# Fourier mixing and a SoLU block on one core: edge columns to GpSimd and ScalarE, and an earlier start for the products of w_in

## The chip, the cores and the metric

The kernel runs on one core of a Trainium2 chip, as one launch. A core has a matrix engine (TensorE, PE in the profile), a vector engine (VectorE, DVE), a scalar engine (ScalarE, ACT), a general engine (GpSimd, POOL) and a fifth (SyncE, SP) that here only issues transfers. They run side by side, each through its own queue, and wait for each other through semaphores. Sixteen DMA engines move data between DRAM and the on-chip memory; transfers issued by SyncE are the queue q1 of the profile, the gathers issued by GpSimd are q0. The metric is the device time of the launch in microseconds (us); lower is better.

## The reference

A real array x of 8 sequences, 3136 positions and 256 features goes through two Fourier transforms, of which the real part is kept. The result, 25088 rows of 256, goes through a SoLU block with a layer norm:

```python
X = np.fft.fft(np.fft.fft(x, axis=1), axis=2).real.astype(np.float32)
h = X.reshape(25088, 256) @ w_in                    # 256 x 1024
e = np.exp(h - np.max(h, axis=-1, keepdims=True))
sm = e / (np.sum(e, axis=-1, keepdims=True) + 1e-09)
solu = h * sm
mu = np.mean(solu, axis=-1, keepdims=True)
var = np.mean((solu - mu) ** 2, axis=-1, keepdims=True)
ln = (solu - mu) / np.sqrt(var + 1e-06) * g_ln
out = (ln @ w_out).astype(np.float32)               # 1024 x 256
```

x and g_ln are float32. w_in and w_out arrive as float64, so the kernel has to turn them into float32 itself.

## The kernel before

**Tiling.** The eight sequences are handled as four pairs (class Pair). The 3136 positions are split into 49 x 64, and the transform along them is done in two steps. `transform1` multiplies by the table F (49 points), `transform2` by the table T (64 points). The symmetry of a real transform is used: x is added to its mirror image along the sequence (`add_mirror`, from a copy xb that GpSimd gathers in reversed order), and then features d and 256-d are added and subtracted into a tile y (`fold_features`). The transform along the features is not done on the data: its table Q is multiplied into w_in beforehand. So the first product of the SoLU block uses Wi = Q x w_in, and w_mid holds one more row for the middle feature.

**Chunks.** A pair is processed in NC = 8 chunks c of CH = 4 positions each. For the first pair (`first`), a chunk is loaded (`load`: xa by SyncE, xb by GpSimd), mirrored and folded whole. The edge columns have no partner in the fold: column 0 gets only the mirror add (L147) and is then copied to y together with column 128 (L165). Chunk 7 also has y0, from position 0. For later pairs the work is spread over the main loop in halves (`fold_part`). The tiles y have two buffers, so the fold of chunk c can start when `transform1` of chunk c-2 has read its y. `transform1` runs twice per chunk: two matmuls (columns 0 to 128, and 129 to 255) into a PSUM bank, then a ScalarE copy (L220) to a tile z. After each chunk, rows of z go to DRAM (zd, by `keep`). When all eight chunks are there, `turn` reads them back as g in another layout, and `transform2` can start. A float32 matmul shows as two records in the profile.

**Weights.** w_in comes in four pieces of 512 KB (`piece_in`): pieces 0 and 1 are its first 128 rows (w_in[0]), 2 and 3 its other 128 rows (w_in[1]). Each is turned from float64 to float32 by integer steps: `exponent_in` takes the exponent on VectorE (L586) and clamps it with three ScalarE activations (`confine`, L610, L612, L614); `narrow_in` builds the float on VectorE (L586, L627, L630, L636). w_out goes the same way later (`exponent_out`, `narrow_out`). `product_in(h, parts)` computes a half h of Wi: parts 0 and 2 are the contributions of w_in[0] to the two column halves, 1 and 3 those of w_in[1]. `keep_in` (L694) copies the finished product out of PSUM on ScalarE. `product_in(KD)` is the product for w_mid, from a table that `mid` prepares. `scale_out` transposes the gain g_ln through PSUM bank 2, and ScalarE copies it out (L711). `mean_out(0)` and `mean_out(1)` sum w_out over its rows on TensorE (L737), for the mean of the layer norm.

**Order.** `tc.manual_schedule()` is in force: every engine executes its instructions in the order in which the program writes them. The start of the program is a hand-written sequence: loads, then the loop over the eight chunks of the first pair, in which the narrowing of the weights is interleaved, then the products that are left, then the second transform of units 0 and 1. A unit is one k1 of one pair. After that the main loop goes over 4 x 25 units: `up` (L281, h), `even` and `join`, `expo`, `product`, `square`, the transposition, and the second product (`down`, or `Down` with seven block products in place of eight). The transfers of the start are issued by SyncE in this order: idx, pieces 0 and 1, xa of chunk 0, F, the gain, piece 2, xa of chunks 1 and 2, piece 3, xa of chunks 3 to 5, Q; then, as buffers come free, xa of chunks 6 and 7, w_out, T and the keeps. The six first gathers of xb are issued by GpSimd meanwhile, before it clears T.

**PSUM.** `result(i)` gives bank i % 4 of four banks. `transform1` of the first pair uses them in turn, two per chunk.

Of the kernel before, what the change touches and what calls it, by code (L numbers as in the profile page):

```python
# [9 lines left out]
FP32 = mybir.dt.float32  # L10
I32 = mybir.dt.int32
U32 = mybir.dt.uint32
ALU = mybir.AluOpType
# [10 lines left out]
PR = 2 * N1  # L24
ZR = 4 * NK
CH = 4
NC = NH // CH
# [17 lines left out]
def kernel(  # L45
# [19 lines left out]
    nc = tc.nc  # L65
    B, S, D = x.shape
    FF = moe_w_in.shape[1]
    KF = FF // P
    KD = D // P
# [8 lines left out]
    xpool = ctx.enter_context(tc.tile_pool(name="xpool", bufs=2))  # L78
# [17 lines left out]
    ident = const.tile([P, P], FP32, name="ident")  # L96
# [9 lines left out]
    def result(i):  # L106

        return banks[i % 4]
# [9 lines left out]
    def load(pr, c, room=None):  # L118

        r = slice(pr.p * PR, (pr.p + 1) * PR)  # L120
        rows = PR if pr.p else P
        if room is None:
            xa = xpool.tile([P, CH, D], FP32, tag="xa", name="xa")
            xb = xpool.tile([P, CH, D], FP32, tag="xb", name="xb")
        else:
            xa, xb = (t.rearrange("p (l d) -> p l d", d=D) for t in room)
        nc.sync.dma_start(out=xa[0:rows], in_=x_pn[r.start : r.start + rows, c * CH + 1 : (c + 1) * CH + 1, :])
        i = pr.p * NC + c
        nc.gpsimd.indirect_dma_start(
            out=xb[0:rows].rearrange("p l d -> p (l d)"), out_offset=None, in_=x_g,  # L130
            in_offset=bass.IndirectOffsetOnAxis(ap=idx[0:rows, i : i + 1], axis=0))
        xa, xb = xa[0:PR], xb[0:PR]
        x0 = None
        if c == NC - 1:
            x0 = xpool.tile([PR, 1, D], FP32, tag="x0", name="x0", bufs=1)
            nc.sync.dma_start(out=x0, in_=x_pn[r, 0:1, :])
        pr.raw[c] = (xa, xb, x0)

    def add_mirror(pr, c, engine, part=None):

        xa, xb, _ = pr.raw[c]
        rows = (0, CH) if part is None else (part * CH // 2, (part + 1) * CH // 2)
        r = slice(rows[0], min(rows[1], CH - 1 if c == NC - 1 else CH))
        a, rb = xa[:, r, :], xb[:, ::-1, :][:, r, :]
        i = engine.tensor_tensor(out=a[:, :, 1:D], in0=a[:, :, 1:D], in1=rb[:, :, D - 1 : 0 : -1], op=ALU.add)  # L145
        if part is None:
            engine.tensor_tensor(out=a[:, :, 0:1], in0=a[:, :, 0:1], in1=rb[:, :, 0:1], op=ALU.add)  # L147
        return i

    def fold_features(o, i):  # L150
        up, down = i[:, :, 1:128], i[:, :, 255:128:-1]
        nc.vector.tensor_tensor(out=o[:, :, 1:128], in0=up, in1=down, op=ALU.add)
        nc.vector.tensor_tensor(out=o[:, :, 129:256], in0=up, in1=down, op=ALU.subtract)

    def fold(pr, c):

        xa, _, x0 = pr.raw.pop(c)
        pr.y[c] = xpool.tile([PR, CH, D], FP32, tag="y", name="y")
        sides = [(pr.y[c], xa)]
        if c == NC - 1:  # L160
            pr.y0 = xpool.tile([PR, 1, D], FP32, tag="y0", name="y0", bufs=1)
            sides.append((pr.y0, x0))
        for o, i in sides:
            fold_features(o, i)
            nc.vector.tensor_copy(out=o[:, :, 0:129:128], in_=i[:, :, 0:129:128])  # L165

    def fold_part(pr, c, part):

# [66 lines left out]
    def transform2(pr, k1, bank=0):  # L235

        i, k = divmod(k1, KG)
        g = pr.g[i]  # L240
        table = T[0][:, :, k, :] if i == 0 else T[1][:, :, k1 - KG, :]
        ps = result(bank)[:, 0 : KD * P]
        for h in range(KD):
            o = ps[:, h * P : (h + 1) * P].rearrange("p (b k) -> p b k", b=2)
            nc.tensor.matmul(o, g[:, k, h * P : (h + 1) * P], table,  # L245
                             start=(h == 0), stop=True, skip_group_check=True)
        return ps
# [324 lines left out]
    NW = 512  # L572
# [25 lines left out]
    def confine(unit, here=False, parts=(0, 1, 2)):  # L598

        if unit is None:  # L600
            return
        if here:
            bits(unit, unit, -896.0, ALU.add, 0.0, ALU.max)
            bits(unit, unit, 255.0, ALU.min, 2.0 ** 23, ALU.mult)
            return

        u = unit.bitcast(FP32)
        for i in parts:
            if i == 0:
                nc.scalar.activation(out=u, in_=unit, func=ACT.Relu, bias=limits[:, 0:1])  # L610
            elif i == 1:
                nc.scalar.activation(out=u, in_=u, func=ACT.Relu, bias=limits[:, 1:2], scale=-1.0)  # L612
            else:
                nc.scalar.activation(out=unit, in_=u, func=ACT.Identity, bias=limits[:, 2:3], scale=-(2.0 ** 23))  # L614
# [24 lines left out]
    class Weights:  # L639
# [43 lines left out]
        def product_in(self, h, parts=range(4), ps=None):  # L683
# [6 lines left out]
                nc.tensor.matmul(ps[:, fs], lhsT, self.w_in[c][:, fs], start=(c == 0), stop=(c == KD - 1))  # L690
            return ps

        def keep_in(self, h, ps):
            nc.scalar.copy(w_mid if h == KD else Wi[:, h, :], ps)  # L694

# [61 lines left out]
    def ahead(pr, i, work, after=None):  # L757

        for c in range(NC):
            a = i - SUMS[pr.p][c]  # L760
            if work == "load" and (i == (pr.p - 1) * NK and c < 2 and (c or pr.p == 1) or a == 2 and c + 2 < NC):
                load(pr, c if a != 2 else c + 2)
            if work == "mirror" and a in (0, 1):
                behind(add_mirror(pr, c, nc.gpsimd, a), after or units[i - 1])
            if work == "fold" and a in (1, 2):
                fold_part(pr, c, a - 1)
# [24 lines left out]
    with tc.manual_schedule():  # L791
        pairs = [Pair(p) for p in range(NP)]
        first, weights = pairs[0], Weights()
# [10 lines left out]
        weights.piece_in(1)  # L804
        load(first, 0)
        nc.sync.dma_start(out=F, in_=f_tab)
        weights.load_gain()
        weights.piece_in(2)
        for c in range(1, 6):
            load(first, c, rooms.get(c))  # L810
            if c == 2:
                weights.piece_in(3)
        weights.load_tables()
        nc.vector.memset(ones, 1.0)
        nc.vector.memset(neg_half, -0.5)
        bits(top_bit, neg_half[:, 0:1].bitcast(I32), 31, ALU.logical_shift_right, 31, ALU.logical_shift_left)
# [6 lines left out]
        for c in range(NC):  # L823

            if c == 0:
                weights.narrow_in(0)
                weights.narrow_in(1)
            elif c == 1:
                weights.narrow_in(2)
            add_mirror(first, c, nc.vector)  # L830
            if c == 0:
                weights.exponent_in(2)
            fold(first, c)
            if c == 1:
                weights.exponent_in(3)
            elif c == 2:
                weights.narrow_in(3)
            if c == NC - 1:
                for i in range(2):
                    weights.exponent_out(i)  # L840
                confine(weights.units[0], True)
                weights.narrow_out(0)
            if c + 6 < NC:
                load(first, c + 6)
            if c == 3:
                weights.place_out()
                for i in range(2):
                    weights.load_out(i)
                weights.load_table(0)
                weights.scale_out()  # L850
            for s in range(CH // 2):
                if c == NC - 1:
                    confine(weights.units[0], parts=(s,))
                transform1(first, c * CH // 2 + s)
            if c == 3:
                weights.mid()
            elif c == 5:
                weights.keep_in(0, weights.product_in(0))
            elif c == 6:
                odd = weights.product_in(1, (0, 1))  # L860

        turn(first, 0, nc.sync, 0, 2)
        turn(first, 0, nc.gpsimd, 2, KG)

        weights.product_in(1, (2, 3), odd)
        middle = weights.product_in(KD)
        confine(weights.units[0], parts=(2,))
        for i in range(2, 4):
            weights.exponent_out(i)
        weights.keep_in(1, odd)  # L870
        confine(weights.units[1])
        weights.keep_in(KD, middle)

        units = [Unit(p, k1) for p in range(NP) for k1 in range(NK)]
        for i in (1, 2):
            weights.narrow_out(i)
        pairs_q = [(t, transform2(pairs[0], t.k1, t.k1)) for t in units[:2]]
        confine(weights.units[0], parts=(0, 1))
        for (t, ps), part in zip(pairs_q, ((2,), ())):
# [29 lines left out]
        def begin(i):  # L909

            cur = units[i]
            enter(i)
            ps = up(cur, 0)
            if i in (2, 3):
                column(cur)
            even(cur, ps)
            cur.odd = up(cur, 1)
            second_transform(i + 2)
# [5 lines left out]

        batches = []
        begin(0)
        weights.mean_out(0)
        for i in range(whole + 1):
            cur = units[i]
            prv = units[i - 1] if i else None  # L930
# [242 lines left out]
```

## Time and profile before

| What | Value |
|---|---|
| median of three runs | 1124.88 us (1123.95 to 1125.96) |
| the profiled execution | 1123.85 us, of which the span is 1122.1 us |
| TensorE busy | 98% of the span |
| VectorE, ScalarE, GpSimd busy | 87%, 71%, 72% |
| TensorE busy from 0 to 15 us | 0 us |
| TensorE busy from 15 to 30 us | 12.3 us |
| first matmul of the first transform | 15.17 us |
| first matmul of the second transform | 51.65 us |

The span is the time from the first to the last instruction in the profile; the launch takes a little more. All times of events below are microseconds from the start of the span. A row of a timeline has the start, the duration, the engine, the line, the operation, output<-input, the number of instructions that were merged into the row, and in brackets how long the engine had been idle before it and what released it. Rows of DMA queues have the number of packets, the megabytes, and the share of the 16 DMA engines' time that they took.

### The profile page before, as it was taken

What the parts mean: (1) busy time and instruction counts of PE and PEld (TensorE: products, weight loads), DVE (VectorE), ACT (ScalarE), POOL (GpSimd) and SP (SyncE); (2) the same over time, 40 slices, a digit from 0 to 9 for tenths busy, and PEclk for the clock granted to TensorE, in tenths of its full rate; (3) what the DMA queues carried; (4) which work ended last, traced back from release to release, by engine and by line L of the source; (5) the groups of instructions that cost most, each with busy time, mean ns of one, the idle gap of its engine ahead of it and who ended that gap; (6) DMA issues with size and microseconds to landing.
All of it is one profiled execution on the core that took longest, in us unless ns stands there. A gap on an engine that the chain in (4) does not pass through costs nothing. (4 is left out here: it accounts for less than half of the span.)

```text
span 1122.1 us, 22005 instructions
## 1 busy us (share of the span) xinstructions
PE 1094.5 (98%) x7031; PEld 874.5 (78%) x7031; DVE 977.8 (87%) x1438; ACT 798.6 (71%) x1946; POOL 803.5 (72%) x709
## 2 busy tenths in 40 slices
PE   4999999999999999999999999999999999999998
PEld 2556878788777788787887787887877788778888
DVE  7889888989889889898889989898988899898884
ACT  4578777777766877777767777777776777777771
POOL 4057888767777879875876788876775676766664
PEclk9999999999999999999999999999999999999999
DMA  9574897766988979766898788876686875965655
GB/s 354 175 196 100 176 194 191 179 148 149 175 173 167 197 177 198 186 148 141 156 179 178 170 180 186 204 180 142 147 159 145 140 163 120 161 138 117 142 131 127
DMA packets 457930, 187.75 MB, mean 167 GB/s; under 512 B 424646, under 2 KB 439254, under 8 KB 457816
## 3 DMA queue, kind: packets, MB, share of 16 engines
q1 hardware_dynamic: 443800, 146.94, 62.2%
q0 software_dynamic: 14016, 39.40, 13.2%
q8 instruction: 57, 0.93, 0.3%
q14 instruction: 57, 0.47, 0.1%
HBM read 46.75 MB, written 38.80 MB: 76 GB/s over the span
## 5 line engine op out<-in xcount | busy, mean ns | idle before, releaser
L281 PE MATMUL ps_h<-Wi,q 128*128 128x512 f32 x800 | 361.6, 593 | 0.8 <-ACT q L251 0.4
L457 POOL TENSOR_TENSOR S<-uT 128x512 f32<-128x512 f32 x186 | 237.4, 1276 | 110.2 <-DVE u L317 30.7
L464 PE MATMUL ps_m<-Ws,S 128*128 128x128 f32 x2304 | 296.0, 275 | 0.0
L464 PEld LDWEIGHTS ps_m<-Ws,S 128*128 128x128 f32 x2304 | 279.5, 192 | 3.2 <-issue 0.2
L324 ACT ACTIVATE h<-u,usum 128x1024 f32<-128x1024 f32 x196 | 225.0, 1149 | 71.6 <-DVE u L317 71.6
L281 PEld LDWEIGHTS ps_h<-Wi,q 128*128 128x128 f32 x800 | 144.3, 190 | 145.4 <-issue 142.2
L317 DVE SCALAR_TENSOR_TENSOR u<-h,u 128x1024 f32<-128x1024 f32 x196 | 233.0, 1224 | 10.5 <-ACT u L310 10.5
L310 ACT ACTIVATE u<-h,nmax 128x1024 f32<-128x1024 f32 x196 | 223.2, 1140 | 2.3 <-DVE nmax L302 1.1
L388 DVE STREAM_TRANSPOSE v<-u 128x2048 f32<-128x2048 f32 x88 | 203.4, 2311 | 3.0
L464 PE MATMUL ps_m<-Wo,uT 128*128 128x128 f32 x1536 | 203.7, 276 | 0.3 <-DMA out_dram<-ot 0.3
L464 PEld LDWEIGHTS ps_m<-Wo,uT 128*128 128x128 f32 x1536 | 187.9, 192 | 1.4 <-issue 1.4
L302 DVE CUSTOM_DVE_ANT_0 h<-ev,ps_h 128x1024 f32<-128x1024 f32 x100 | 122.1, 1221 | 17.4 <-DVE ev L294 9.1
L302 DVE CUSTOM_DVE_ANT_0 h<-h,ps_h 128x1024 f32<-128x1024 f32 x96 | 117.2, 1221 | 14.2 <-ACT ot L508 0.5
L551 POOL DMA_INDIRECT out_dram<-ot,idx x96 | 107.3, 1118 | 28.4 <-issue 11.1
L294 DVE SCALAR_TENSOR_TENSOR ev<-w_mid,r,ps_h 128x1024 f32<-128x1024 f32 x99 | 122.8, 1240 | 2.7 <-PE ps_h L281 2.6
L457 POOL TENSOR_TENSOR S<-uT,S 128x512 f32<-128x512 f32 x93 | 118.8, 1277 | 7.2
L457 POOL TENSOR_TENSOR S<-S,uT 128x512 f32<-128x512 f32 x93 | 118.6, 1276 | 7.3
L464 PE MATMUL ps_m<-Ws,uT 128*128 128x128 f32 x768 | 101.8, 276 | 0.0
L464 PE MATMUL ps_m<-Wo,S 128*128 128x128 f32 x768 | 101.4, 275 | 0.0
L245 PEld LDWEIGHTS ps_m<-T,g 128*128 128x128 f32 x400 | 60.0, 191 | 49.3 <-issue 47.9
L499 ACT ACTIVATE ot<-ps_m,rs 128x256 f32<-128x256 f32 x96 | 45.5, 474 | 70.3 <-PE ps_m L464 50.3
L145 POOL TENSOR_TENSOR xa<-xa,xb 98x510 f32<-98x510 f32 (+1 forms) x48 | 59.5, 1240 | 48.0 <-DVE u L317 43.7
(111 smaller groups left out, 1244.0 us busy)
## 6 DMA issues: line engine op xcount, KB each, us to landing
uT<-v SPq DMA_DIRECT2D x752, 128.0 KB
g<-zd POOLq DMA_DIRECT2D x72, 160.0 KB, 5.3
out_dram<-ot SPq DMA_DIRECT2D x176, 64.0 KB
zd<-z SPq DMA_DIRECT2D x24, 400.0 KB
xa<-in_x_dram SPq DMA_DIRECT2D x24, 392.0 KB
raw_in<-in_moe_w_in_dram SPq DMA_DIRECT2D x4, 512.0 KB
xa<-in_x_dram SPq DMA_DIRECT2D x4, 512.0 KB
room<-in_x_dram SPq DMA_DIRECT2D x4, 512.0 KB
```

Source lines behind the costliest of these rows:

```text
L145: i = engine.tensor_tensor(out=a[:, :, 1:D], in0=a[:, :, 1:D], in1=rb[:, :, D - 1 : 0 : -1], op=ALU.add)
L245: nc.tensor.matmul(o, g[:, k, h * P : (h + 1) * P], table, start=(h == 0), stop=True, skip_group_check=True)
L281: nc.tensor.matmul(ps[:, fs], t.q[:, c * P : (c + 1) * P], Wi[:, c, fs], start=True, stop=not whole_even)
L294: nc.vector.scalar_tensor_tensor(out=t.ev, in0=w_mid, scalar=t.r, in1=ps, op0=ALU.mult, op1=ALU.add)
L302: nc.vector.tensor_tensor_reduce(out=t.h[s], in0=t.h[0] if s else t.ev, in1=t.odd, scale=1.0 if s else -0.5, scalar=3.0e38, op0=ALU.add, o ...
L310: nc.scalar.activation(out=t.u[s], in_=t.h[s], func=ACT.Exp, bias=t.nmax[:, s : s + 1], scale=-1.0, accum_out=t.esum[:, s : s + 1])
L317: t.last = nc.vector.scalar_tensor_tensor(out=t.u[s], in0=t.h[s], scalar=-1.0, in1=t.u[s], op0=ALU.mult, op1=ALU.mult, accum_out=t.usum[:, ...
L324: nc.scalar.activation(out=t.h[s], in_=t.u[s], func=ACT.Square, bias=t.usum[:, s : s + 1], scale=-float(FF), accum_out=t.ssq[:, s : s + 1])
L388: nc.vector.transpose(out=t.batch.v[:, :, t.w], in_=t.both.rearrange("p s (g n) -> p (s g) n", n=32))
L457: i = engine.tensor_tensor(out=S[j], in0=a, in1=b, op=op)
L464: nc.tensor.matmul(o, a[:, c], b[:, c], start=start and c == 0, stop=c == n - 1, skip_group_check=True)
L551: dma = nc.gpsimd.indirect_dma_start(out=out, out_offset=bass.IndirectOffsetOnAxis(ap=idx[:, i : i + 1], axis=0), in_=t.ot[s], in_offset=None)
```

## The change

Four things are changed, all before the main loop.

- **Edge columns of the first pair.** The small mirror add of column 0 in place on VectorE is removed. `fold` instead has GpSimd add column 0 of xa and xb straight into y, and has ScalarE copy column 128. The VectorE copy of both columns goes away. The extra rows of chunk 7 and the columns of y0 are copied by ScalarE.
- **Q.** Its load is issued right behind F's, ahead of the gain, piece 2 and the later chunks.
- **Products of w_in.** Parts 0 and 2 of both halves of Wi are computed ahead of the first transform of chunk 0. Parts 1 and 3 follow after chunks 3 and 4, each with its copy by ScalarE. Before, half 0 was computed whole after chunk 5, and half 1 in two portions after chunks 6 and 7. A new function `busy(i, n)` issues n matmuls of 256 columns whose result in bank i is overwritten: 2, 4, 2 and 5 of them, ahead of chunks 0, 1, 2 and 3.
- **mean_out(0)** moves ahead of the second transforms of units 0 and 1; it stood behind the first `begin`.

```diff
@@ add_mirror
         i = engine.tensor_tensor(out=a[:, :, 1:D], in0=a[:, :, 1:D], in1=rb[:, :, D - 1 : 0 : -1], op=ALU.add)
-        if part is None:
-            engine.tensor_tensor(out=a[:, :, 0:1], in0=a[:, :, 0:1], in1=rb[:, :, 0:1], op=ALU.add)
         return i
@@ fold
-        xa, _, x0 = pr.raw.pop(c)
-        pr.y[c] = xpool.tile([PR, CH, D], FP32, tag="y", name="y")
-        sides = [(pr.y[c], xa)]
+        xa, xb, x0 = pr.raw.pop(c)
+        y = pr.y[c] = xpool.tile([PR, CH, D], FP32, tag="y", name="y")
+        n = CH - 1 if c == NC - 1 else CH
+        nc.gpsimd.tensor_tensor(out=y[:, 0:n, 0:1], in0=xa[:, 0:n, 0:1], in1=xb[:, ::-1, :][:, 0:n, 0:1], op=ALU.add)
+        nc.scalar.copy(y[:, :, 128:129], xa[:, :, 128:129])
+        fold_features(y, xa)
         if c == NC - 1:
+            nc.scalar.copy(y[:, n:, 0:1], xa[:, n:, 0:1])
             pr.y0 = xpool.tile([PR, 1, D], FP32, tag="y0", name="y0", bufs=1)
-            sides.append((pr.y0, x0))
-        for o, i in sides:
-            fold_features(o, i)
-            nc.vector.tensor_copy(out=o[:, :, 0:129:128], in_=i[:, :, 0:129:128])
+            nc.scalar.copy(pr.y0[:, :, 0:129:128], x0[:, :, 0:129:128])
+            fold_features(pr.y0, x0)
@@ class Weights
+        def busy(self, i, n):
+            for _ in range(n):
+                nc.tensor.matmul(result(i)[:, 0 : NW // 2], ident, self.w_in[0][:, 0 : NW // 2], start=True, stop=True)
+
@@ loads
         nc.sync.dma_start(out=F, in_=f_tab)
+        weights.load_tables()
         weights.load_gain()
         weights.piece_in(2)
...
                 weights.piece_in(3)
-        weights.load_tables()
@@ loop over the chunks of the first pair
+            if c < 4:
+                weights.busy(2 * c, (2, 4, 2, 5)[c])
+            if c == 0:
+                made = [weights.product_in(h, (0, 2)) for h in range(KD)]
             for s in range(CH // 2):
                 if c == NC - 1:
                     confine(weights.units[0], parts=(s,))
                 transform1(first, c * CH // 2 + s)
             if c == 3:
                 weights.mid()
-            elif c == 5:
-                weights.keep_in(0, weights.product_in(0))
-            elif c == 6:
-                odd = weights.product_in(1, (0, 1))
+            if c in (3, 4):
+                weights.keep_in(c - 3, weights.product_in(c - 3, (1, 3), made[c - 3]))
 
         turn(first, 0, nc.sync, 0, 2)
         turn(first, 0, nc.gpsimd, 2, KG)
 
-        weights.product_in(1, (2, 3), odd)
         middle = weights.product_in(KD)
...
-        weights.keep_in(1, odd)
         confine(weights.units[1])
         weights.keep_in(KD, middle)
@@ before the second transforms of units 0 and 1
         for i in (1, 2):
             weights.narrow_out(i)
+        weights.mean_out(0)
         pairs_q = [(t, transform2(pairs[0], t.k1, t.k1)) for t in units[:2]]
@@ before the main loop
         begin(0)
-        weights.mean_out(0)
```

## The prediction

> **What bounds the kernel now.** I read the page's busy shares and slices first, then the timelines of TensorE, VectorE, ScalarE and SyncE up to 62 us, then the transfers in one microsecond of the start.
>
> ```profile
> PE 1094.5 (98%) x7031; PEld 874.5 (78%) x7031; DVE 977.8 (87%) x1438; ACT 798.6 (71%) x1946; POOL 803.5 (72%) x709
> ...
> PE   4999999999999999999999999999999999999998
> ```
>
> TensorE is idle for 27.6 us of the span, nearly all of it in the first slice. After that it never stops. So the time is the moment at which TensorE starts on units 0 and 1, plus its own work from there on. The change touches only that start.
>
> ```profile
> 15.17 3.73 PE L217 MATMUL ps_m<-y,F 98*100 98x258 f32 x8 [15.17 <-DVE y L165]
> ...
> 29.01 7.26 PE L217 MATMUL ps_m<-y,F 98*100 98x258 f32 x24 [1.14 <-DVE y L165]
> 36.11 3.60 PE L690 MATMUL wps<-w_in,Q 128*128 128x512 f32 x8
> 39.55 1.89 PE L217 MATMUL ps_m<-y,F 98*100 98x258 f32 x8
> ...
> 51.65 1.13 PE L245 MATMUL ps_m<-T,g 128*128 128x128 f32 x8 [1.16 <-ACT w_mid L694]
> ...
> 57.21 1.89 PE L737 MATMUL ps_m<-Wo,ones 128*128 128x256 f32 x8
> ```
>
> A chunk is 8 matmul records: 3.73 us at 15 us, 1.89 at 40 us (1.72 of issue, 0.215 a record, when the next work follows at once). TensorE is slow until about 32.8 us, in the x24 row. From 29 to 45 us it is the bound: chunks 3 to 7 with products of w_in between them. The last copy of chunk 7 leads through DRAM (zd, g) to the second transform at 51.65.
>
> ```profile
> 41.48 0.59 ACT L220 COPY S<-ps_m 100x512 f32<-100x512 f32 x1 [0.23 <-PE ps_m L217]
> ...
> 45.37 0.59 ACT L220 COPY z_g<-ps_m 100x512 f32<-100x512 f32 x1
> ```
>
> A copy out of PSUM starts 0.2 us after the last matmul and takes 0.59. The second row is the end of chunk 7; 51.65 - 45.37 = 6.28 us from there to the second transform.
>
> ```profile
> 20.79 0.43 DVE L586 TENSOR_SCALAR S<-raw_in 128x512 int32<-128x512 int32 x1 [0.51 <-DMA raw_in<-in_moe_w_in_dram]
> ...
> 26.18 1.22 DVE L145 TENSOR_TENSOR room<-room 98x1020 f32<-98x1020 f32 x1
> ```
>
> VectorE waits for the last quarter of w_in (piece 3), which lands at 20.8; chunk 3's mirror add starts 5.39 later.
>
> ```profile
> q0 software_dynamic: 67, 0.27, 66.4%
> q1 hardware_dynamic: 71, 0.13, 34.8%
> ```
>
> These are the transfers from 26.5 to 27.5 us, when Q went beside the gathers of x. The queues moved about as many records each, not as many bytes. A gather's record (4 KB) took 0.664 x 16 / 67 = 0.16 us. Q's rows (1028 B) took about 0.045: of q1's 5.6 engine-us some 21 records are 4 KB at 0.16.
>
> [...] at 45.86 ScalarE starts a clamp whose operand had been ready since 45.27, behind the z_g copy. [...] L165 at 19.98 took 0.30 instead of 0.17 and ended with a gather's issue on GpSimd.
>
> **The change part by part.**
>
> *Edge columns.* Per chunk VectorE loses L147 (0.16) and L165 (0.17); as they are pipelined, 0.16 from start to start, 1.3 us over eight chunks. Only that of chunk 2 counts below, since VectorE waits for data before it and for buffers after it. GpSimd's add of 4 columns isn't in the trace. I bound it by 0.2 (a memset) and 1.04 (L379, four elements, a power) and take 0.3. It runs as soon as x lands and a y buffer is free, with GpSimd idle until 48.5, and holds one gather by as much: hidden. ScalarE's copy is 0.19 (L178). It reads a column that the mirror add writes, and in the built program it stands behind the copies of the chunk before, and TensorE's chunk waits for it. That place is the cost of this change.
>
> *Q behind F.* Q has 256 rows, 16 to each of 16 engines. If each takes turns with one gather record: 16 x (0.16 + 0.045) = 3.3, and 3.4 with the slower records of this stage. Pieces 2 and 3 and x behind it come 3.4 later, while the gathers come sooner. By bytes alone it would be 257 KB at the 200 GB/s of one of two queues, 1.3 us. I take 3.4. Piece 3 lands at 24.2 instead of 20.8, and VectorE, which has nothing to do then, passes that on. Piece 2 goes from 13.1 to 16.5: chunk 0's fold ends about 18.2.
>
> *Products and dummy matmuls in front.* Two dummies (0.86 each, slow) at 9.5, then four matmuls of 1.71 from Q's landing, near 14. [...] products end at 19.5 to 20.9, chunk 0 at 21.2 to 22.6. With four dummies (1.72) chunk 1 starts near 23.5, and two more go before chunk 2. All of this lies beside VectorE's waits. In the order of ScalarE chunk 2 starts after the clamps of piece 3: harmless.
>
> *Chunk 3.* Its five dummies write the PSUM bank of the gain's transpose, so they wait for ScalarE's g_ln copy, which stands behind chunk 3's edge copy, which waits for chunk 3's mirror add. From piece 3: 5.39 - 0.15 to that add, 1.22 + 0.04 for it, 0.19 edge copy, 0.08 g_ln (0.18, overlapped), 0.08 handing over, ten records of 0.215 = 2.15. Sum 9.0. Chunk 3 starts at 33.2, before 29.0.
>
> *Chunks 3 to 7.* Chunk 3 takes 1.72 and its product half (four records of 0.43) 1.72. Then ScalarE: 0.2, 1.01 for the copy of the product, 0.19 for chunk 4's edge copy, less 0.1 overlap, and hand-over with weight load 0.17: TensorE stands for 1.5. From chunk 3 to chunk 4, 4.9; chunk 4 to 5, the same 4.9. From 5 to 6 and 6 to 7: 1.72 and 0.2 + 0.59 - 0.1 + 0.19 + 0.17 = 1.05, so 2.8 each. Chunk 7 to its last copy 2.5. Sum 9.8 + 5.6 + 2.5 = 17.9, at 51.1; before 45.37. Delta +5.7, where the products' first halves moved out of this stretch should have won.
>
> *Behind it.* VectorE's folds of chunks 6 and 7 wait for a y buffer that TensorE frees two chunks earlier; w_out's narrowing starts near 46.6 instead of 39.4. TensorE's middle product ends at 54.5 (3.43 from 51.0). mean_out(0) needs the second narrowing, about 54.3, and takes 1.73. The second transform comes 6.28 after 51.1, at 57.4: both are covered, by 1.2 us; if narrowing is later than that, it costs the excess. What stood at 57.21 in TensorE's full stretch is gone: -1.73, since VectorE waits 1.87 there for TensorE (L294 at 60.86).
>
> **Sum.** +5.7 - 1.7 = +4.0. The profiled execution was 1123.85 (span 1122.1); this becomes 1127.9. The runs' median, 1124.88, is 1.0 above that execution: 1128.9.
>
> **The rivals.**
> *Shares by bytes.* Q costs 1.3: piece 3 at 22.1, everything 2.1 earlier, +1.9: 1126.8. Against it: the counts above. The early stage has slower records, which makes the cost larger if anything.
> *TensorE is not held by ScalarE.* This one ends faster. If edge copies are done ahead of their chunk, chunk 3 to the last copy is 0.12 + 6 x 1.72 + 2.38 = 12.8 us and not 17.9. With Q at 3.4 the end is at 46.0: +0.6 - 1.7, 1123.8, no change that counts. With Q at 1.3 it is at 43.9: -1.5 - 1.7 = -3.2, 1121.7. Speaks for it: ScalarE is busy for only 1.3 of 5 us from 25 to 30. Against it: it isn't load but order; the copy stands behind one that waits for TensorE. It decides if the four holds, 5.1 us together, come to less than about 1 us with the cheaper Q.
> *Narrowing gets late.* VectorE and ScalarE meet in the clamps of w_out; 2 us more than counted would show: 1131.
> *The dummies don't speed TensorE up.* Chunks then take 3.43; [...] I give it no weight of its own.
>
> **How the numbers follow.** The likeliest, slower by 4.0, has 0.5, and its own range is 1127.2 to 1130.6. Late narrowing 0.08, Q by bytes 0.15 (a part of it over the bound), ScalarE doesn't hold 0.27, of which 0.18 is faster and the rest no change. What can be told from no change is about 0.2%, 2.25 us: faster than 1122.6 has 0.19, within 0.21, slower 0.6. The range leaves out the fast end and the worst of late narrowing: 1123 to 1131.
>
> **What would show it.** Right: VectorE's L586 of w_in idle till about 16.5 and 24 on raw_in; dummies ahead of chunk 3 starting only after its mirror add; in TensorE's timeline gaps of 1 to 1.5 us ahead of chunks 4 to 7, released by ScalarE; last z_g copy near 51; second transform near 57. Wrong: piece 3 before 22.5, gaps under 0.5 us, or z_g before 46. The changed kernel's L741 must lie ahead of L245, or the 1.73 isn't won.

## The result

The changed kernel takes 1128.89 us in the median of seven runs (1126.84 to 1130.1), the kernel before 1124.88 in seven (1123.95 to 1125.96). The ratio is 1.0033, with a 95% interval of 1.0021 to 1.0044: slower, by 4.0 us between the medians. The profiled execution took 1126.84 us with a span of 1125.0, 3.0 and 2.9 more than before.

The busy shares and TensorE's slices of the changed kernel:

```profile
PE 1097.8 (98%) x7057; PEld 877.0 (78%) x7057; DVE 975.4 (87%) x1421; ACT 799.3 (71%) x1956; POOL 810.6 (72%) x717
...
PE   5899999999999999999999999999999999999998
```

TensorE starts earlier (first slice 5, was 4) and is then less dense (second slice 8, was 9); from the third on nothing differs. It is busy for 3.3 us more in all, and its 26 more matmul records are those of the 13 dummies (the matmuls of `busy`, whose results nothing reads); VectorE, ScalarE and GpSimd hardly changed: the shares don't tell what happened.

TensorE's timeline of the changed kernel:

```profile
13.79 6.53 PE L690 MATMUL wps<-w_in,Q 128*128 128x512 f32 x8 [1.94 <-DMA Q<-in_q_tab_dram]
20.16 1.89 PE L217 MATMUL ps_m<-y,F 98*100 98x258 f32 x8
...
27.93 1.94 PE L217 MATMUL ps_m<-y,F 98*100 98x258 f32 x8 [1.56 <-ACT y L159]
...
31.04 2.43 PE L695 MATMUL ps_m<-w_in,ident 128*128 128x256 f32 x10 [1.01 <-ACT g_ln L715]
33.30 1.89 PE L217 MATMUL ps_m<-y,F 98*100 98x258 f32 x8
35.03 1.88 PE L690 MATMUL wps<-w_in,Q 128*128 128x512 f32 x4
38.16 1.94 PE L217 MATMUL ps_m<-y,F 98*100 98x258 f32 x8 [1.25 <-issue]
...
43.07 1.94 PE L217 MATMUL ps_m<-y,F 98*100 98x258 f32 x8 [1.25 <-issue]
45.83 1.94 PE L217 MATMUL ps_m<-y,F 98*100 98x258 f32 x8 [0.82 <-issue]
48.59 2.40 PE L217 MATMUL ps_m<-y,F 98*100 98x258 f32 x16 [0.82 <-issue]
...
54.26 1.89 PE L741 MATMUL ps_m<-Wo,ones 128*128 128x256 f32 x8
57.31 1.16 PE L245 MATMUL ps_m<-T,g 128*128 128x128 f32 x8 [1.17 <-DMA g<-zd]
58.49 3.70 PE L281 MATMUL ps_h<-Wi,q 128*128 128x512 f32 x8
```

TensorE begins with two dummies and the products, and chunk 0 follows at 20.16 instead of 15.17, but at full speed (1.89 us, where a chunk took 3.73 before). Chunk 3 starts at 33.30 instead of 29.01. Then there is a gap ahead of each of chunks 4 to 7, where TensorE had none before. The second transform is at 57.31 instead of 51.65. mean_out (L741) stands ahead of it without a wait.

What the gaps wait for is read from ScalarE's timeline, since "issue" names no releaser:

```profile
36.95 1.01 ACT L698 COPY Wi<-wps 128x1024 f32<-128x1024 f32 x1 [0.54 <-PE wps L690]
37.86 0.20 ACT L159 COPY y<-room 98x4 f32<-98x4 f32 x1
39.27 0.58 ACT L220 COPY z_v<-ps_m 100x512 f32<-100x512 f32 x1 [1.21 <-PE ps_m L217]
...
51.02 0.58 ACT L220 COPY z_g<-ps_m 100x512 f32<-100x512 f32 x1
...
58.06 0.37 ACT L251 COPY q<-ps_m 128x256 f32<-128x256 f32 x1 [1.22 <-PE ps_m L245]
```

The copy of four columns (L159) of chunk 4 ends at 38.06 and TensorE starts chunk 4 at 38.16. It stands behind the 1.01 us copy of Wi, which itself waits for TensorE's product. VectorE had done its part of that y at 34.61. ScalarE's own idle time before the z copies shows that this is order, not load.

VectorE's timeline of the changed kernel: the arrival of the last two pieces of w_in and the first uses of h:

```profile
16.50 0.43 DVE L586 TENSOR_SCALAR S<-raw_in 128x512 int32<-128x512 int32 x1 [2.42 <-DMA raw_in<-in_moe_w_in_dram]
...
24.05 0.46 DVE L586 TENSOR_SCALAR S<-raw_in 128x512 int32<-128x512 int32 x1 [0.90 <-DMA raw_in<-in_moe_w_in_dram]
...
60.55 1.28 DVE L294 SCALAR_TENSOR_TENSOR ev<-w_mid,r,ps_h 128x1024 f32<-128x1024 f32 x1 [0.71 <-PE ps_h L281]
...
64.39 1.28 DVE L294 SCALAR_TENSOR_TENSOR ev<-w_mid,r,ps_h 128x1024 f32<-128x1024 f32 x1
```

The same two uses of h in the kernel before, and its first `up`:

```profile
55.30 1.28 DVE L294 SCALAR_TENSOR_TENSOR ev<-w_mid,r,ps_h 128x1024 f32<-128x1024 f32 x1 [0.72 <-PE ps_h L281]
...
60.86 1.28 DVE L294 SCALAR_TENSOR_TENSOR ev<-w_mid,r,ps_h 128x1024 f32<-128x1024 f32 x1 [1.87 <-PE ps_h L281]
```

```profile
53.23 3.70 PE L281 MATMUL ps_h<-Wi,q 128*128 128x512 f32 x8 [0.44 <-ACT q L251]
```

Piece 3 is taken up at 24.05, 3.26 us later than before. L294 of the first unit is 5.25 later, that of the second only 3.53: the 1.72 between them are the four matmuls of mean_out(0) that no longer stand there. From there the distance holds through the whole main loop: the last L294 starts at 1084.60, before at 1081.11, 3.49 later. The other 0.6 that the profiled executions lack is at the very end. There TensorE waited for an output transfer before, and does not now; this row is the kernel before, the next the changed one:

```profile
1110.75 1.18 PE L464 MATMUL ps_m<-Wo,uT 128*128 128x128 f32 x8 [0.32 <-DMA out_dram<-ot]
```

```profile
1113.96 1.18 PE L464 MATMUL ps_m<-Wo,uT 128*128 128x128 f32 x8
```

The distance of the last matmuls is 3.2, and that of the spans, behind the last output transfer, 2.9. I take these 0.6 for chance of two executions, not for a gain of the change.

### The profile page after: what moved, and what is told of

The parts are those of the page before. It is cut to its first block, busy times and chain, and to the rows that moved or that the text cites. A ratio compares the mean times of both kernels' runs of the same rounds, so it can differ in the third digit from the quotient of the medians.

```text
span 1125.0 us, 22091 instructions
## 1 busy us (share of the span) xinstructions
PE 1097.8 (98%) x7057; PEld 877.0 (78%) x7057; DVE 975.4 (87%) x1421; ACT 799.3 (71%) x1956; POOL 810.6 (72%) x717
## 5 line engine op out<-in xcount | busy, mean ns | idle before, releaser
L551 POOL DMA_INDIRECT out_dram<-ot,idx x96 | 110.7, 1154 | 27.9 <-issue 12.4
L294 DVE SCALAR_TENSOR_TENSOR ev<-w_mid,r,ps_h 128x1024 f32<-128x1024 f32 x99 | 122.8, 1241 | 0.9 <-PE ps_h L281 0.7
```

The source lines that it names most:

```text
L294: nc.vector.scalar_tensor_tensor(out=t.ev, in0=w_mid, scalar=t.r, in1=ps, op0=ALU.mult, op1=ALU.add)
L551: dma = nc.gpsimd.indirect_dma_start(out=out, out_offset=bass.IndirectOffsetOnAxis(ap=idx[:, i : i + 1], axis=0), in_=t.ot[s], in_offset=None)
```

## The experiments

All ratios are to the kernel before, run beside each kernel on the same chip, with the 95% interval. "Profiled" is the time of the one profiled execution of each kernel.

| Kernel | Median us | Ratio | Profiled us |
|---|---|---|---|
| changed kernel | 1128.89 | 1.0033 [1.0021, 1.0044] | 1126.84 |
| e1_edges_vector | 1121.05 | 0.9965 [0.9952, 0.9979] | 1121.05 |
| e2_q_early_in_before | 1128.71 | 1.0031 [1.0019, 1.0043] | 1128.64 |
| e3_mean_early_in_before | 1123.12 | 0.9983 [0.9974, 0.9991] | 1122.97 |
| f1_q_gpsimd | 1125.67 | 1.0004 [0.9995, 1.0012] | 1125.7 |
| f2_both_repaired | 1119.58 | 0.9951 [0.9937, 0.9964] | 1119.56 |
| f4_no_dummies_chunk3 | 1127.6 | 1.0024 [1.0014, 1.0033] | 1126.93 |
| g1_changed_again | 1128.9 | 1.0035 [1.0023, 1.0047] | 1126.47 |
| g2_more_dummies_chunk2 | 1126.73 | 1.0017 [1.0009, 1.0025] | 1127.38 |
| g4_changed_third (one run) | 1127.4 | - | 1127.4 |
| v1_all_out_of_the_way | 1118.67 | 0.995 [0.9937, 0.9964] | 1118.01 |
| f6_v1_no_dummies | 1119.72 | 0.9948 [0.9934, 0.9961] | 1120.19 |
| g3_v1_filled | 1118.51 | 0.9943 [0.993, 0.9957] | 1119.25 |

**Do the small copies on ScalarE hold TensorE?** In the changed kernel, ScalarE's share of the edge copies goes back to VectorE, behind the fold; GpSimd's add stays.

```diff
-        nc.scalar.copy(y[:, :, 128:129], xa[:, :, 128:129])
         fold_features(y, xa)
+        nc.vector.tensor_copy(out=y[:, :, 128:129], in_=xa[:, :, 128:129])
         if c == NC - 1:
-            nc.scalar.copy(y[:, n:, 0:1], xa[:, n:, 0:1])
+            nc.vector.tensor_copy(out=y[:, n:, 0:1], in_=xa[:, n:, 0:1])
...
-            nc.scalar.copy(pr.y0[:, :, 0:129:128], x0[:, :, 0:129:128])
             fold_features(pr.y0, x0)
+            nc.vector.tensor_copy(out=pr.y0[:, :, 0:129:128], in_=x0[:, :, 0:129:128])
```

> The changed kernel, with the copy of column 128 (and those of chunk 7's last row and of y0) on VectorE behind the fold instead of on ScalarE ahead of it. Theory (ScalarE's order holds TensorE ahead of chunks 4 to 7): the gaps of 1.25, 1.25, 0.82 and 0.82 us go, chunk 3 starts 0.9 us earlier, the last z_g copy comes at 45.5 instead of 51.0 us. mean_out(0) then waits for w_out's narrowing and gives 0.9 us back: 4.6 us under the changed kernel, about 1124.3. Rival (piece 3's late landing is the cause, and the fold on VectorE the bound): at most 0.9 us, about 1128, and the gaps stay, released by VectorE.

It measured 1121.05 us, 0.9965. TensorE's timeline of this kernel:

```profile
32.09 1.94 PE L217 MATMUL ps_m<-y,F 98*100 98x258 f32 x8
33.87 1.88 PE L690 MATMUL wps<-w_in,Q 128*128 128x512 f32 x4
35.59 1.89 PE L217 MATMUL ps_m<-y,F 98*100 98x258 f32 x8
37.31 1.88 PE L690 MATMUL wps<-w_in,Q 128*128 128x512 f32 x4
39.03 5.89 PE L217 MATMUL ps_m<-y,F 98*100 98x258 f32 x32
...
51.59 1.16 PE L245 MATMUL ps_m<-T,g 128*128 128x128 f32 x8 [0.39 <-DMA g<-zd]
```

All four gaps are gone, and chunks 4 to 7 follow each other at 1.72 us. The last z copy starts at 45.33, where 45.5 was expected. The 0.9 us that mean_out(0) was expected to give back did not show: it waited 0.85 us for the narrowing, but was done before g arrived, and the second transform came 5.7 us earlier, as the z copy did. The profiled execution is 5.8 us shorter than that of the changed kernel, by the ratios it is 7.7 (1.0033 - 0.9965, of 1125). So the order on ScalarE costs more than the whole slowdown; the 1.9 between the two figures comes up again below.

**What does Q's place cost?** First alone, in the kernel before:

```diff
         nc.sync.dma_start(out=F, in_=f_tab)
+        weights.load_tables()
         weights.load_gain()
...
-        weights.load_tables()
```

> The kernel before, with Q's load behind F's and nothing else. Theory (Q's rows take turns with the gathers record by record): piece 3 lands 3.3 us later (24.0 instead of 20.8), chunk 3's mirror add and everything behind it move by about that, 1128.1. Rival (by bytes): piece 3 at 22.1, 1126.2. Second rival (the first slice has slack for it): 1124.9.

It measured 1128.71 us, 1.0031. VectorE's timeline and then TensorE's of this kernel:

```profile
16.10 0.43 DVE L586 TENSOR_SCALAR S<-raw_in 128x512 int32<-128x512 int32 x1 [2.82 <-DMA raw_in<-in_moe_w_in_dram]
...
23.77 0.43 DVE L586 TENSOR_SCALAR S<-raw_in 128x512 int32<-128x512 int32 x1 [0.80 <-DMA raw_in<-in_moe_w_in_dram]
```

```profile
32.00 7.66 PE L217 MATMUL ps_m<-y,F 98*100 98x258 f32 x24 [1.14 <-DVE y L165]
...
56.62 5.40 PE L281 MATMUL ps_h<-Wi,q 128*128 128x512 f32 x8 [0.18 <-ACT q L251]
```

Piece 3 comes 3.0 us later and chunk 3 starts 3.0 later, all of it from the place of one transfer of 257 KB, and not the 1.3 that its bytes would take (an estimate: 257 KB at half of the 0.40 MB that both queues moved from 26.5 to 27.5 us in the kernel before). The last row is something else: the same eight records took 3.70 in the kernel before. The granted clock in this execution was half from 57.07 to 60.48 us (0.57 in the mean from 57 to 61).

Then the other way: the changed kernel with Q issued by GpSimd, in the queue of the gathers.

```diff
-            nc.sync.dma_start(out=self.Q, in_=q_tab.rearrange("(c p) d -> p c d", p=P))
+            nc.gpsimd.dma_start(out=self.Q, in_=q_tab.rearrange("(c p) d -> p c d", p=P))
```

> The changed kernel with Q loaded through GpSimd's queue behind the first gather, nothing else. Theory (Q's place ahead of piece 2 costs 3.3 us through piece 3, and the holds by ScalarE stay): piece 3 no longer stops VectorE, everything from chunk 3 on comes 3.3 to 3.6 us earlier, the gaps of 1.25 and 0.82 us ahead of chunks 4 to 7 stay; last z_g copy at 47.5, 1125.4. Rival (the holds alone are the cost, and Q's delay is absorbed): 1128.9.

It measured 1125.67 us, 1.0004, as expected. But its profile doesn't show all of the way there. VectorE takes up piece 3 at 20.74, as early as in the kernel before. TensorE's timeline of this kernel:

```profile
26.49 1.94 PE L217 MATMUL ps_m<-y,F 98*100 98x258 f32 x8
...
31.54 1.89 PE L217 MATMUL ps_m<-y,F 98*100 98x258 f32 x8
...
36.40 1.94 PE L217 MATMUL ps_m<-y,F 98*100 98x258 f32 x8 [1.25 <-issue]
```

Chunk 3 gains only 1.76, since TensorE's own row is next late: the first products (6.69 us, 6.53 in the changed kernel) end where they ended before, chunk 0 starts at 20.32 (20.16), and dummies and chunks 0 to 2 follow without a gap. ScalarE's gap is unchanged. Of the profiled execution 1.1 us is gone, of the median 3.2.

**Both repaired**: the two edits above together.

> The kernel of the first run (edge columns on VectorE) with Q loaded through GpSimd's queue behind the first gather. Theory: the two costs add, as they lie in one chain; last z_g copy at 41.9 instead of 45.3, 3.5 us under that run: 1117.6. Rival (the folds on VectorE set the pace once the holds are gone, or w_out's narrowing holds mean_out): 1119 to 1121.

It measured 1119.58 us, 0.9951: the rival's number, for another reason than it gave. The last z copy is at 43.13 instead of 41.9. As in f1 it is TensorE's queue that is next late, not VectorE. What Q's place costs thus depends on what lies beside it: 3.0 us at chunk 3 in the kernel before, 1.8 in the changed one. Once the edges are on VectorE, 1.6 by the ratios and 1.5 between the profiled executions is left; the intervals of the two ratios overlap.

**What does the early mean_out(0) gain?** It alone, in the kernel before:

```diff
             weights.narrow_out(i)
+        weights.mean_out(0)
         pairs_q = [(t, transform2(pairs[0], t.k1, t.k1)) for t in units[:2]]
...
         begin(0)
-        weights.mean_out(0)
```

> The kernel before, with mean_out(0) ahead of the second transforms of units 0 and 1 and nothing else. Theory: its 1.73 us lie in the wait for g, behind the middle product (49.7 to 51.4) and the second narrowing (48.3), and the first up of unit 1 comes 1.7 us earlier: 1123.2. Rival (VectorE or the ScalarE chain behind unit 0 sets the pace there): 1124.9.

It measured 1123.12 us, 0.9983, a gain of 1.9. TensorE's timeline of this kernel:

```profile
51.40 1.89 PE L737 MATMUL ps_m<-Wo,ones 128*128 128x256 f32 x8
53.13 1.05 PE L245 MATMUL ps_m<-T,g 128*128 128x128 f32 x8
```

The four matmuls lie where TensorE waited for w_mid's copy and g before; the second transform follows at once. In this execution TensorE was at full clock from 25.02 us, fell back to half at 28.44 and was at full again from 35.26; its row of chunks 3 to 5 took 8.62 us instead of 7.26, and the next row began 1.07 later than before. L294 of the first unit is late by the same 1.07 (56.37), that of the second early by 0.65 (60.21): 1.72 between them. The move is a gain of its own, shown apart from the rest.

**The dummies, and the 2 us between profile and median.** First the five dummies ahead of chunk 3 are left out:

```diff
-            if c < 4:
-                weights.busy(2 * c, (2, 4, 2, 5)[c])
+            if c < 3:
+                weights.busy(2 * c, (2, 4, 2)[c])
```

> The changed kernel without the five dummy matmuls ahead of chunk 3. Theory (they cost there, since TensorE is at full clock since 19.5 us and they wait for ScalarE's g_ln): chunk 3 starts when its fold is done, at 31.5 instead of 33.2, and everything behind it follows, 1127.2. Rival (they keep the clock): TensorE is idle from 29.8 to 31.5, falls to half clock, and chunks 3 and 4 with their products cost 1.7 us each more: 1129 to 1131.

It measured 1127.6 us, 1.0024, not told apart from the changed kernel. TensorE's timeline of this kernel, and the busy time by stretches (stretch; its length; busy time of TensorE, its weight load, VectorE, ScalarE, GpSimd with counts; granted clock; DMA share; GB/s):

```profile
27.64 2.33 PE L217 MATMUL ps_m<-y,F 98*100 98x258 f32 x8 [1.72 <-ACT y L159]
...
31.31 3.71 PE L217 MATMUL ps_m<-y,F 98*100 98x258 f32 x8 [1.14 <-DVE y L150]
```

```profile
28.00:32.00 4.00, 2.86 (x11) 1.72 (x10) 3.83 (x6) 1.34 (x4) 0.22 (x1) 0.63 0.89 340
32.00:36.00 4.00, 4.00 (x10) 2.55 (x9) 3.73 (x5) 1.53 (x4) 0.27 (x1) 0.51 0.72 217
```

Both theories are seen at once. Chunk 3 starts 2 us earlier, as the first says; and the granted clock has fallen to half, as in the rival, though already after the gap of 1.72 ahead of chunk 2, so that the chunk takes 3.71 and the gain is gone. TensorE had been at full clock before (1.89 us for chunk 1 at 23.16). (The record of the granted clock begins where TensorE first comes to full, at 19.52 us in the changed kernel and 32.80 in the kernel before. That it is at half before that is read from the durations: 3.73 us a chunk, 3.71 in the fall here.)

That made me ask what the gap ahead of chunk 2 does in the changed kernel. In the records, the granted clock changes on a grid of 3.41 us: it was at half for 3.41 us in e2 and for twice that in e3, and the 1088.85 us at full clock in the kernel before (32.80 to 1121.65) are 319 times 3.413. A stretch from one point of this grid to the next is called a window here. Windows with 1.61 us of idle time in e2, 1.72 in f4, 1.85 in f6 and 1.86 in e3 were followed by half clock; one with 1.56 in the changed kernel and one with 1.61 in the kernel before were not. So about half a window idle was enough in these four. Where the grid lies against the gap differs between executions: full clock came at 19.52 us in the changed kernel and, by an estimate below, near 16.2 in g1. So a gap can fall into one window or be split over two. The next two runs are the changed kernel unaltered, and with that gap filled by four more dummies:

```diff
-                weights.busy(2 * c, (2, 4, 2, 5)[c])
+                weights.busy(2 * c, (2, 4, 6, 5)[c])
```

> The changed kernel again, unaltered, for a second profile and times beside the two that follow. Theory (in part of its executions TensorE falls back to half clock[...]): the time is again near 1128.9, spread over 3 us, and a profile of an execution near the median or above shows a granted clock near 0.5 somewhere between 26 and 37 us; one at 1127 or below doesn't. Rival (the spread comes from the main loop, as the kernel before has it): no such fall in a profile at 1128.5 or more.

> The changed kernel with six dummies ahead of chunk 2 instead of two, which fill the idle time that TensorE has there (26.2 to 27.9 us). Theory (the clock falls in part of the executions): no falls, the executions lie near the fastest ones of the changed kernel, 1126.8 to 1127.5. Rival (no falls, or no cost): the four dummies end at 27.95, 0.1 us late at most, 1128.9.

The unaltered kernel measured 1128.9 us (1126.47 to 1132.07, nine runs), 1.0035; the filled one 1126.73 (1125.97 to 1127.62, fifteen runs), 1.0017. TensorE's timeline of g1 and then of g2:

```profile
27.53 1.94 PE L217 MATMUL ps_m<-y,F 98*100 98x258 f32 x8 [2.38 <-ACT y L159]
```

```profile
25.85 2.75 PE L695 MATMUL ps_m<-w_in,ident 128*128 128x256 f32 x12
28.73 1.94 PE L217 MATMUL ps_m<-y,F 98*100 98x258 f32 x8
```

The filled kernel does more and starts chunk 2 later; its profiled execution is 0.9 us longer than that of g1. Yet its median is 2.2 lower, and its runs spread over 1.65 us instead of 5.6. So the executions profiled of the changed kernel aren't typical of it. e1 and f1 agree: they too shorten the gap ahead of chunk 2 (to 0.95 us and to nothing), their profiled execution equals their median within 0.03 us, and each gains about 2 us more in the median than in the profile (7.7 against 5.8; 3.2 against 1.1). In g1 the gap of 2.38 us lay across two windows by an estimate, about 1.3 us in the first and 1.1 in the second: its products took 5.25 us against 6.53 in the changed kernel, so twice the 1.28 us of difference was no longer at half clock, full clock came near 16.2, and a point of the grid lay near 26.4. The clock stayed (1.00 from 24 to 32 us).

The changed kernel was profiled a third time:

> The changed kernel once more, unaltered, for a third profile. Theory (TensorE falls back to half clock in part of the executions): if this one takes 1128.5 us or more, its granted clock is near 0.5 for some microseconds between 26 and 37 us; at 1127 or less it stays at 1.00 there. Rival: 1128.5 or more with the clock at 1.00 throughout.

It took 1127.4 us, with a gap of 1.28 and full clock. None of the three profiles of this kernel has a fall, and none was of an execution above 1127.4. But the mean granted clock of every execution is on record, profiled or not. In the profiled executions it is 0.997 or 0.998 in the four with a fall (e2, e3, f4, f6) and 0.999 or 1.000 in the ten without; one window of 3.41 us at half clock is 0.0015 of the span, and what is lost after TensorE's last work is at most 0.001. Sorted by it (a fall is 0.998 or less):

| Kernel | Executions | with a fall | their median us | median us of the others |
|---|---|---|---|---|
| kernel before (beside the experiments) | 67 | 39 | 1125.71 | 1124.61 |
| changed kernel (first runs, g1, g4) | 17 | 10 | 1129.18 | 1127.40 |
| f4, no dummies ahead of chunk 3 | 12 | 10 | 1127.98 | 1127.48 |
| e1, f1, g2: gap under 1 us, none, filled | 33 | 0 | - | 1121.05, 1125.67, 1126.73 |

In the changed kernel the two kinds don't overlap: 1126.47 to 1127.9 us without a fall, 1128.48 to 1132.07 with one. So the falls are shown, 1.8 us at the median, and g2 shows their cause: with the gap ahead of chunk 2 filled, and nothing else altered, none of 15 executions fell. In which microseconds the clock was at half the mean doesn't tell. The kernel before falls as often, but there it parts the times less, by 1.1 us at the median and with ranges that overlap. One fall there need not cost much: e3's execution, which fell, came to lasting full clock at 35.26, and the profiled one of the kernel before, which did not, came to full clock for the first time at 32.80.

**A version in which nothing stands in the way.** Q by GpSimd; both edge columns of a chunk by one GpSimd operation straight from x; eight dummies ahead of chunk 0 only; first halves of the products ahead of chunk 1, second halves ahead of chunk 3.

```diff
+        nc.gpsimd.tensor_tensor(out=y[:, 0:n, 0:129:128], in0=xa[:, 0:n, 0:129:128],
+                                in1=xb[:, ::-1, :][:, 0:n, 0:129:128], op=ALU.add)
...
             if c == 0:
+                weights.busy(0, 8)
+            elif c == 1:
                 made = [weights.product_in(h, (0, 2)) for h in range(KD)]
+            elif c == 3:
+                for h in range(KD):
+                    weights.keep_in(h, weights.product_in(h, (1, 3), made[h]))
```

> The changed kernel with the costs taken out: Q loaded through GpSimd's queue behind the first gather, so that it doesn't take turns with the gathers; columns 0 and 128 both added by GpSimd from the raw x, the mirror add leaving them out, no edge copy on ScalarE; eight dummies ahead of chunk 0 and no others; first halves of the products ahead of chunk 1, second halves ahead of chunk 3. Theory: VectorE doesn't wait for pieces 2 and 3, its last fold ends near 37.6, the last z_g copy comes near 40.3, mean_out(0) gives back up to 1.8 us: 1118 to 1120. Rival (a gather or GpSimd's add gets late and holds VectorE, or TensorE is late from the products): 1122 or more.

It measured 1118.67 us, 0.995. TensorE's timeline of this kernel:

```profile
10.05 6.53 PE L701 MATMUL ps_m<-w_in,ident 128*128 128x256 f32 x16 [10.05 <-DVE w_in L642]
16.42 1.89 PE L223 MATMUL ps_m<-y,F 98*100 98x258 f32 x8
18.15 3.60 PE L696 MATMUL wps<-w_in,Q 128*128 128x512 f32 x8
...
47.74 1.13 PE L251 MATMUL ps_m<-T,g 128*128 128x128 f32 x8 [0.55 <-DMA g<-zd]
```

The same products that took 6.53 us in the changed kernel, at half clock up to 19.52, take 3.60 here, behind dummies. VectorE now works without a wait from 12.3 to 50.7 us and sets the pace of the chunks. Ahead of chunks 4 and 5 the profile names GpSimd's add (0.52 and 0.51 us), but VectorE's folds of the same chunks (L157) end at 33.65 and 36.20, behind TensorE's starts at 33.18 and 35.74, and the two rows take 2.06 and 2.05 us. Two kernels asked what the dummies and a remaining gap are worth: f6 leaves the eight dummies out, g3 puts two dummies before mean_out(0) and one behind it.

> The version with everything out of the way, without its eight dummies ahead of chunk 0. Theory: TensorE begins at 15.3 at half clock, chunk 0 and most of the first product halves take twice as long, the delay is caught up only in part by chunk 7, 1 to 2 us more: 1120.3. Rival (VectorE is the bound anyway): 1118.7.

> The version with everything out of the way, with two dummies more between the middle product and mean_out(0), where TensorE waits 1.2 us for w_out's narrowing, and one behind mean_out(0), where it waits 0.55 us for g. Theory (the clock falls there in part of the executions, as the profile of the version without dummies showed at 49 us): executions near the fastest of that version, 1118.0 to 1118.4. Rival (it doesn't fall with this little idleness): 1118.7 to 1119.0.

They measured 0.9948 and 0.9943. Neither can be told from v1, nor from f2. In f6's profile the last z copy is 1.06 later (42.37), and a fall to half clock follows at 49.29; its time is inconclusive. By the mean clock two of five executions of v1 fell, three of six of f6 and none of five of g3. All four (f2, v1, f6, g3) beat both kernels, by 5.5 to 6.4 us against the kernel before; f2 is the smallest edit of the changed kernel that does.

## Why the prediction was right, and where not

**Right, and shown.**

| Step | Predicted | Measured |
|---|---|---|
| piece 2, piece 3 taken up | 16.5, 24.2 | 16.50, 24.05 |
| first products start | near 14 | 13.79 |
| chunk 1, chunk 3 | 23.5, 33.2 | 23.61, 33.30 |
| chunk 3 to 4, 4 to 5 | 4.9 each | 4.86, 4.91 |
| chunk 5 to 6, 6 to 7 | 2.8 each | 2.76 each |
| last z_g copy | 51.1 | 51.02 |
| narrowing of w_out starts | 46.6 | 46.82 |
| second transform | 57.4 | 57.31 |
| early mean_out(0) | -1.73 | -1.72 |

The cause is the one that had half the chance: a small copy that stands in ScalarE's order behind one that waits for TensorE (e1), in a stretch already delayed by Q (e2). Turns by record were the right price for Q: 3.0 to 3.3 us measured, 3.4 taken. The rival by bytes fell with piece 3 at 24.05, in place of the 22.1 that its 1.3 us would give. The rival in which TensorE isn't held fell with the gaps of 0.8 to 1.25. Late narrowing fell too, since mean_out(0) did not wait. GpSimd's add of four columns, bounded by 0.2 and 1.04, took 0.21 to 0.90 us; it held ScalarE's copy for chunk 3 by less than 0.1 us and nothing else.

**Wrong: the sum, though its total agrees with the median.** "+5.7 - 1.7 = +4.0" in the kernel's own time is 0.4 too much. Behind the second transform the q copy on ScalarE no longer waits behind a clamp: `up` follows it after 1.18 us instead of 1.58 (58.49 - 57.31, and 53.23 - 51.65). So the chain is +5.25 - 1.72 = +3.5, which is what the main loop carries to its end, and the profiled execution is +3.0.

**Wrong: "the runs' median, 1124.88, is 1.0 above that execution", carried over as a constant.** It isn't one. The changed kernel's median lies 2.05 above its profiled execution (2.4 in g1). The profiled executions had no fall, and five of the seven timed ones had. The prediction asked whether the dummies bring TensorE to full clock. That they would, and when, was the author's estimate; with them and the products in front it came at 19.52 us (1.89 us a chunk from 20.16 on), and what of it is due to the dummies was not shown apart in this kernel. It didn't ask whether TensorE keeps full clock. It put chunk 2 "after the clamps of piece 3: harmless", and that wait is the gap in which the clock falls (10 of 17 executions, and none of 15 with the gap filled, in g2). The kernel before falls too (39 of the 67 executions beside the experiments), so the 1.0 carried over will have held falls already; what it lacked is that in the changed kernel a fall costs some 0.7 us more (1.8 against 1.1). With the gap filled, as in g2, about 2 us of the 4.0 go by the ratios. That 1128.9 was met to the tenth is therefore luck in part: some 1 us too much in the chain and its end, and as much too little for the clock.

**Open.** The place of the fall within an execution of the changed kernel rests on g2, since no execution with a fall was profiled. Why a fall costs less in the kernel before was argued from one profile and not tested. The products moved ahead were not run alone. f2 keeps them, the dummies, GpSimd's add and the early mean_out(0), and is 5.5 us faster than the kernel before by the ratio; mean_out(0) alone gave 1.9, and the other 3.6 are not divided further.

## What to carry to other kernels

A tiny operation moved to an idle engine is not free because the engine is idle: ask what stands ahead of it in that engine's order, and whether that waits for the very consumer (in e1, with the small copies on VectorE, the profiled execution was 5.8 us shorter). A transfer of small rows, put ahead in a queue that shares its engines with another busy queue, cost its number of records in turns here and not its bytes (3.0 us in e2, where 1.3 was the estimate by bytes); in the other queue it cost the late pieces nothing (piece 3 at 20.74 in f1, 20.79 in the kernel before). When idle gaps are cut or filled by dummies, sort the executions by their mean granted clock and compare like with like: one profile can miss a loss that most executions have (here 1.8 us, in 10 of 17).

## What the runs showed of the hardware beyond that

In four profiles, 1.61 to 1.86 us without TensorE work in one window of 3.41 us were enough for half clock (1.61 in the kernel before were not), for one window in e2 (57.07 to 60.48) and f6, and for two in f4 and e3 (28.44 to 35.26 in e3). Full clock came back at 60.48 in e2 and at 35.26 in e3, each time after a window for which TensorE's timeline shows no idle time; windows with 0.10 and 0.19 us early in e2 and one with 0.28 in e3 (28.44 to 28.72) did not bring it.

The turns between the two DMA queues went by single records: 3.3 us for Q's 16 rows on each engine is 0.2 a turn. Equal counts alone (119 and 120 records from 25 to 27 us of the kernel before) don't show the order; the starts and ends of the records do. Strung together so that one record begins where another ends, which gives the order on each engine, in these 2 us the next record was of the other queue in 174 cases and of the same queue in 20.
